# q and k of the later batches: cast on ACT, through a DRAM scratch, read back by transposing DMAs

## The chip, the cores and the metric

The kernel runs on one core of a Trainium2 chip. The metric is the time of one execution on the device in microseconds; the median of several runs is given with the lowest and the highest. A profile records one more execution, instruction by instruction; its span runs from the first instruction to the last and is a little shorter than the time of that execution.

The core has five engines with a queue of instructions each. PE (TensorE) multiplies matrices and loads weights (PEld); DVE (VectorE), ACT (ScalarE) and POOL (GpSimd) work on elements; SP (SyncE) here only issues DMAs. POOL issues DMAs too. An engine takes the instructions of its queue in order: if one waits, all behind it wait.

## The reference

A sliding-window attention, whose output feeds a two-layer network with an ELU between the layers. There are 8 batches, 8 heads, 576 positions, head size 64 and 2048 hidden units; everything is float32 outside.

```python
scores = scale * np.matmul(q, k.transpose(0, 1, 3, 2))
mask = np.abs(pos[:, None] - pos[None, :]) <= 32
attn = softmax(np.where(mask, scores, -1000000000.0))
attn_out = np.matmul(attn, v)                       # (8, 8, 576, 64)
x = attn_out.transpose(0, 2, 1, 3).reshape(4608, 512)
h = x @ w_in                                        # 512 -> 2048
g = np.where(h > 0.0, h, np.exp(np.minimum(h, 0.0)) - 1.0)
out = g @ w_out                                     # 2048 -> 512
```

## The kernel before, in words

**Attention.** The positions of a batch are cut into nine blocks of 64 queries; the 72 blocks of the eight batches are taken in 36 pairs. A block needs only 128 keys around it, so its scores are one 128 x 64 tile a head. For that, q and k must lie with the head dimension across the partitions. `qT` and `kT` hold them so, as bf16, four pairs of heads side by side, two buffers each, used by even and odd batches. `kT` has 32 zero columns on each side of each head pair's 576 keys.

A pair goes through `scores` (L245: 16 matmuls, then an exp on ACT), `mask` (L262, DVE), `pv` (L271, 16 matmuls with V in `V_e` or its copy shifted by 64 rows, `V_o`), `normalize` (L285, DVE) and a transpose of the result `x_st` into `xT`. The first eight pairs do this last transpose on PE (`x_transpose`, `x_evac`), the others with a transposing DMA on SP's queue (`x_dma`, L315).

**How qT and kT are filled.** `load_qk` (L102) brings q or k of a batch into a float32 tile `f` of 96 partitions, six positions a partition, on SP's queue; there are two such tiles for q and two for k. `cast_qk` (L209) casts one pair of heads to bf16. `transpose_qk` (L221) then transposes it on PE, six times 96 x 128 into one PSUM bank, and an engine copies the bank into `qT` or `kT`. Batches 0 and 1 do this in halves, with casts on DVE and ACT. For batches 2 to 7 (L414 to L423) the cast of each head pair runs on POOL and the evacuation on ACT: eight casts, eight groups of six transposes and eight evacuations a batch.

**V and the weights.** POOL's queue issues the loads of V (`load_v`, L114, five DMAs a batch, which cast to bf16 on the way, three buffers) and of the weights. `rotate_v` (L122) makes `V_o` out of `V_e` with two DMAs on SP's queue.

**The network.** Tokens are taken in 18 tiles of 256, that is two pairs each. A tile has eight steps, and a step has two hidden blocks of 128: `mm1` (L439, eight matmuls of 256 columns, exp on ACT into `e_sb`, minus one on DVE into `m_sb`), `elu` (L458, DVE, into `g_sb`) and `mm2` (L466, four matmuls of 512 columns that add into `psY`). After the last step of a tile, ACT and DVE copy `psY` to `y_sb`, and SP's queue stores it.

**The order of work.** It is written out by hand: the program runs through 144 steps `kk`, and the attention's parts are entered into a table by step and slot. A step of the loop at L487 does, in this order: `elu` of the step before, slot `dve`, `mm1`, slot `mid`, `mm2` of two steps before, slot `end`. That is the order on each engine's queue. From pair 8 on, `scores` of pair `i` is in step 4(i-2)-2, only pair 8 is in step 24; `pv` follows one step later at the end, `normalize` and the x transpose two steps later. The tile's `mm1` starts at step 8t, four steps after its second pair's x transpose was entered.

For batch `b`, `k0` is four times (its first pair minus 2): 28, 44, 64, 80, 100 and 116 for batches 2 to 7. The PE transposes of a head pair are in steps k0-16 to k0-3, two every four steps, and the casts five steps ahead of them; batch 2 has its eight transposes in steps 18 to 25. The loads of `f` of batches 3 to 7 are in steps k0-32 and k0-31, of batch 3 in 18 and 19; the V loads follow one step later, and `rotate_v` is in step k0-4.

Of the kernel before, what the change touches and what calls it, by code (L numbers as in the profile page):

```python
# [10 lines left out]
BF16 = mybir.dt.bfloat16  # L11
# [10 lines left out]
def kernel(  # L22
# [9 lines left out]
    nc = tc.nc  # L32

    B, H, S, D = q.shape
    WIN = 32
# [5 lines left out]
    QB = 64  # L41
    NQB = S // QB
    NPAIR = B * NQB // 2
    HP = H // 2
    SJ = 6
    SP_ = S // SJ
    VS = 5
    VD = D + 1
    KW = S + 2 * WIN

    TT = 256
    NT = N_TOK // TT
# [4 lines left out]
    HALF = STEPS // 2  # L57
# [4 lines left out]
    cpool = ctx.enter_context(tc.tile_pool(name="const", bufs=1))  # L62
    wpool = ctx.enter_context(tc.tile_pool(name="weights", bufs=1))
    lpool = ctx.enter_context(tc.tile_pool(name="loads", bufs=2))
    apool = ctx.enter_context(tc.tile_pool(name="attn", bufs=2))
    xpool = ctx.enter_context(tc.tile_pool(name="xT", bufs=4))
    mpool = ctx.enter_context(tc.tile_pool(name="moe", bufs=3))
    opool = ctx.enter_context(tc.tile_pool(name="outs", bufs=2))


    psum = ctx.enter_context(
# [13 lines left out]
    def ps_tile(shape, dt, tag, name):  # L85
        return pools[tag].tile(shape, dt, tag=tag, name=name)

    qT = [cpool.tile([128, HP, S], BF16, name=f"qT{i}") for i in range(2)]
    kT = [cpool.tile([128, HP, KW], BF16, name=f"kT{i}") for i in range(2)]
    V_e = [cpool.tile([128, VS, H, VD], BF16, name=f"Ve{i}") for i in range(3)]  # L90
    V_o = [cpool.tile([128, VS - 1, H, VD], BF16, name=f"Vo{i}")
           for i in range(3)]
# [6 lines left out]
    WHOLE, HALF_A, HALF_B = (0, SJ), (0, SJ // 2), (1, SJ // 2)  # L99
    qk_f = {}  # L100
# [51 lines left out]
    for i in range(3):  # L152
        nc.vector.memset(V_e[i][:, :, :, D:VD], 1.0)
        nc.vector.memset(V_e[i][0:32, 0], 0.0)
        nc.vector.memset(V_e[i][96:128, VS - 1], 0.0)
        if i < 2:
            nc.vector.memset(kT[i][:, :, 0:WIN], 0.0)
            nc.vector.memset(kT[i][:, :, KW - WIN:KW], 0.0)

    ident = cpool.tile([128, 128], BF16)  # L160
    make_identity(nc, ident)
# [4 lines left out]
    for m in (1, 2, 0, 3, 4):  # L166
# [10 lines left out]
        out=masks, in_=masks, compare_op=ALU.is_ge, fill=0.0,  # L177
        base=0, pattern=[[0, 5], [-1, QB]], channel_multiplier=1)
    nc.gpsimd.affine_select(
        out=masks, in_=masks, compare_op=ALU.is_ge, fill=0.0,  # L180
        base=2 * WIN, pattern=[[0, 5], [1, QB]], channel_multiplier=-1)
    for mi in (0, 4):
        nc.gpsimd.affine_select(
            out=masks[:, mi, :], in_=masks[:, mi, :], compare_op=ALU.is_ge,
            fill=0.0, base=-WIN, pattern=[[0, QB]], channel_multiplier=1)
    nc.gpsimd.affine_select(
        out=masks[:, 3, :], in_=masks[:, 3, :], compare_op=ALU.is_ge,
# [15 lines left out]
    def copy_on(eng, d_, s_):  # L203
        if eng is nc.scalar:
            nc.scalar.copy(d_, s_)  # L205
        else:
            eng.tensor_copy(d_, s_)  # L207

    def cast_qk(b, which, part, hps, eng):  # L209
# [8 lines left out]
        qk_b[b, which, z, hp0] = t  # L218
        copy_on(eng, _bap(t, [t.ap[0], [D, nh], [nh * D, nj], [1, D]]), s_)

    def transpose_qk(b, which, part, hps, evac, tag="t0"):  # L221
        z, nj = part
        src = qk_b.pop((b, which, z, hps[0]))
        nh = len(hps)
        W = 512 if nh > 1 else 1024
        pt = ps_tile([128, nh, W], BF16, tag, "ptx")
        for g in range(nh):
            for j in range(nj):
                nc.tensor.transpose(  # L229
                    pt[:, g, j * SP_:(j + 1) * SP_],  # L230
                    src[:, j, g * 128:(g + 1) * 128], ident[0:SP_, 0:SP_])
        n = SP_ * nj
        if which == 0:
            T, c0 = qT[b % 2], z * n
        else:
            T, c0 = kT[b % 2], WIN + z * n
        d = T[:, hps[0]:hps[0] + nh, c0:c0 + n]
        pitch = d.ap[1][0] if nh > 1 else n
        copy_on(evac,
                _bap(d, [d.ap[0], [pitch, nh], [nj, SP_], [1, nj]]),  # L240
                _bap(pt, [pt.ap[0], [W, nh], [1, SP_], [SP_, nj]]))
# [3 lines left out]
    def scores(i, tag="s"):  # L245
        psS = ps_tile([128, 2, 512], FP32, tag, "psS")
        for z in range(2):
            jb = 2 * i + z
            b, qb = jb // NQB, jb % NQB
            for h in range(H):  # L250
                hp, base = h // 2, 64 * (h % 2)
                nc.tensor.matmul(  # L252
                    psS[:, h % 2, hp * 128 + z * QB:hp * 128 + (z + 1) * QB],
                    lhsT=kT[b % 2][base:base + 64, hp, QB * qb:QB * qb + 128],
                    rhs=qT[b % 2][base:base + 64, hp, QB * qb:QB * (qb + 1)],
                    start=True, stop=True)
        pu = apool.tile([128, H, 2 * QB], BF16, tag="pu")
        nc.scalar.activation(  # L258
            pu, _bap(psS, [psS.ap[0], [1, 1024]]), AX.Exp, scale=SCALE)
        st[i] = [psS, pu, None, None, tag]  # L260
# [59 lines left out]
    def first_pair(b):  # L320
        return NQB * b // 2
# [49 lines left out]
    def at(kk, slot, fn, *args):  # L371
        tasks.setdefault((kk, slot), []).append((fn, args))
# [5 lines left out]
    def pair_at(i, kk):  # L378
        at(kk, "mid", scores, i)
        at(kk + 1, "dve", mask, i)  # L380
        at(kk + 1, "end", pv, i)
        at(kk + 2, "dve", normalize, i)
        at(kk + 2, "end", x_transpose, i)
        at(kk + 3, "dve", x_evac, i)


    for i, tag in ((2, "s"), (3, "u")):
        at(0, "mid", scores, i, tag)
        at(1, "dve", mask, i)
# [7 lines left out]
    for part, kq in ((HALF_A, 8), (HALF_B, 16)):  # L397
        for which in range(2):
            at(kq - 1, "mid", cast_qk, 1, which, part, allh,
               (nc.scalar, nc.vector)[which])  # L400
            at(kq + which, "mid", transpose_qk, 1, which, part, allh,
               nc.scalar, "s")
# [4 lines left out]
    for i in range(8, NPAIR):  # L407
        kk = 24 if i == 8 else HALF * (i - 2) - 2
# [4 lines left out]
        at(kk + 2, "end", x_dma, i)  # L413
    for b in range(2, B):  # L414
        k0 = HALF * (first_pair(b) - 2)
        for n in range(2 * HP):
            if b == 2:
                which, hp, kk, ahead = n // HP, n % HP, 18 + n, 2
            else:
                which, hp = n % 2, n // 2  # L420
                kk, ahead = k0 - 16 + HALF * hp + which, 5
            at(kk - ahead, "mid", cast_qk, b, which, WHOLE, (hp,), nc.gpsimd)
            at(kk, "mid", transpose_qk, b, which, WHOLE, (hp,), nc.scalar)  # L423
        at(k0 - HALF, "mid", rotate_v, b)
        if b >= 3:
            kk = max(k0 - 8 * HALF, 18)
            at(kk, "mid", load_qk, b, 0, WHOLE)
            at(kk + 1, "mid", load_qk, b, 1, WHOLE)
            for m in range(VS):
                at(kk + 2 + m // 3, "mid", load_v, b, m)  # L430
# [97 lines left out]
```

The softmax here doesn't subtract the row's maximum and nothing guards it: scores larger than these inputs give would overflow.

## Time and profile before

| | |
|---|---|
| median of 3 runs | 342.21 us (341.41 to 343.56) |
| profiled execution | 341.63 us, its span 339.9 us |
| PE busy | 308.7 us (91% of the span), 3296 matmuls |
| DVE, ACT, POOL busy | 246.2, 167.3 and 84.3 us |
| PE transposes of q and k | 384, casts of them on POOL 48 of 883 ns |
| evacuations of these on ACT | 52 of 634 ns (128 x 576) |
| casts of 96 x 768 on ACT | 4 of 829 ns |
| hardware queue of SP | 36.25 MB, software queue of POOL 8.92 MB |
| load of q or k of a whole batch | 1152 KB, 9.8 and 9.4 us to landing |
| x transpose by DMA | 28, landing 3.4 us after issue in the median |

How to read it: a line of the profile names the source line (L229), the engine, the tile written and the tiles read. The chain that ended last is followed back from the last instruction, at each step to what released it. Matmuls overlap in the pipeline, so the duration of one is longer than the distance to the next; the chain shows distances. A digit in the slices is the busy share of a fortieth of the span in tenths. The time that a DMA takes to land counts from its issue.

### The profile page before, as it was taken

The page shows a single profiled execution, that of the slowest core. Times are in us where ns is not written, and L with a number is a line of the kernel's source. Part 1 is how long each engine was busy: PE and PEld are TensorE (multiplying, and loading weights), DVE is VectorE, ACT ScalarE, POOL GpSimd, SP SyncE. Part 2 cuts the span into 40 slices and gives each one's busy share as a digit, 9 for nine tenths or more (in the row PEclk, how much of TensorE's full clock was granted, in tenths as well). Part 3 has the DMA queues.
Part 4 walks back from the last instruction along what each step waited for, and adds up shares of the span by engine and source line. Part 5 has one row for each costly group of instructions (what it writes and reads, how often), then busy time and mean ns, then how long its engine had stood idle before and what let it go on. Part 6 is the DMA issues. An engine that isn't in the chain of part 4 may idle for free.

```text
span 339.9 us, 8051 instructions
## 1 busy us (share of the span) xinstructions
PE 308.7 (91%) x3296; PEld 207.4 (61%) x3296; DVE 246.2 (72%) x446; ACT 167.3 (49%) x262; POOL 84.3 (25%) x108
## 2 busy tenths in 40 slices
PE   0347999799799999999999999999999999999994
PEld 0235666566566666666666666666666666666662
DVE  5346667678787777778877888788867777878663
ACT  1624264566545554555555554555555553444331
POOL 8352410085661344034400354021100000000000
PEclk9999999999999999999999999999999999999999
DMA  8999999999998995771949994963202320202011
GB/s 163 187 227 214 218 169 185 218 305 214 131 143 173 216 119 121 174 168 23 188 65 206 178 158 83 225 155 80 79 18 78 80 79 17 77 17 80 15 64 62
DMA packets 79176, 45.67 MB, mean 134 GB/s; under 512 B 53796, under 2 KB 73252, under 8 KB 79140
## 3 DMA queue, kind: packets, MB, share of 16 engines
q1 hardware_dynamic: 37412, 36.25, 47.4%
q0 software_dynamic: 41728, 8.92, 37.9%
q8 instruction: 26, 0.43, 0.6%
q14 instruction: 10, 0.08, 0.1%
HBM read 36.70 MB, written 9.44 MB: 136 GB/s over the span
## 4 chain that ended last, share of the span: by engine, by line
PE 83%; DVE 7%; DMA 4%; ACT 3%; issue 1%; SPq 0%; DVEq 0%
PE ps L447 36%; PE psY L474 35%; PE ptx L229 5%; PE psS L279 4%; PE psS L252 3%; DMA f<-in_k_dram 2%; DVE g_sb L460 2%; DMA Vo<-Ve 2%; DVE m_sb L455 1%; ACT e_sb L453 1%; DVE x_st L291 1%; ACT pu L258 1%; ACT qkb L205 1%; DVE pm L267 1%; DVE xT L313 1%
## 5 line engine op out<-in xcount | busy, mean ns | idle before, releaser
L453 ACT ACTIVATE e_sb<-ps 128x512 f32<-128x512 f32 x144 | 86.0, 597 | 152.1 <-PE ps L447 151.9
L447 PE MATMUL ps<-xT,w_in_sb 128*128 128x256 bf16 x1152 | 150.5, 274 | 4.1 <-DVE xT L313 3.3
L474 PE MATMUL psY<-w_out_sb,g_sb 128*128 128x512 bf16 x576 | 148.0, 379 | 0.2 <-DVE g_sb L460 0.2
L447 PEld LDWEIGHTS <-w_in_sb 128*128 128x128 bf16 x1152 | 110.2, 98 | 41.2 <-issue 4.8
L455 DVE TENSOR_SCALAR m_sb<-e_sb 128x512 bf16<-128x512 f32 x144 | 71.9, 500 | 59.2 <-ACT e_sb L453 58.8
L460 DVE SCALAR_TENSOR_TENSOR g_sb<-ps,m_sb 128x512 bf16<-128x512 f32 x144 | 99.4, 690 | 13.0
L474 PEld LDWEIGHTS <-g_sb 128*128 128x128 bf16 x576 | 50.8, 98 | 38.0 <-DVE g_sb L460 0.7
L207 POOL CAST qkb<-f 96x768 bf16<-96x768 f32 x48 | 41.3, 883 | 120.0 <-DMA f<-in_q_dram 40.0
L118 POOL DMA_DIRECT2D Ve<-in_v_dram x40 | 34.8, 875 | 28.1 <-PE psS L279 13.6
L229 PE MATMUL ptx<-ident,qkb 96*128 96x96 bf16 x384 | 27.7, 215 | 15.0 <-DVE qkb L207 12.5
L258 ACT ACTIVATE pu<-psS 128x1024 bf16<-128x1024 f32 x36 | 36.5, 1019 | 2.7 <-PE psS L252 2.6
L229 PEld LDWEIGHTS <-qkb 96*128 96x128 bf16 x384 | 23.5, 102 | 17.3 <-DVE qkb L207 13.0
L267 DVE TENSOR_TENSOR pm<-pu,masks 128x1024 bf16<-128x1024 bf16 x36 | 26.0, 721 | 2.0 <-ACT pu L258 1.7
L291 DVE TENSOR_TENSOR x_st<-psS,rc 128x512 bf16<-128x512 f32 x36 | 24.9, 692 | 1.2
L279 PEld LDWEIGHTS <-pm 128*64 128x64 bf16 x576 | 12.5, 113 | 17.3 <-DVE pm L267 13.4
L205 ACT COPY qT<-ptx 128x576 bf16<-128x576 bf16 (+1 forms) x30 | 20.0, 666 | 4.1 <-PE ptx L229 4.1
L252 PE MATMUL psS<-qT,kT 64*128 64x64 bf16 x576 | 15.3, 196 | 2.7 <-DVE x_st L291 1.2
L205 ACT COPY kT<-ptx 128x576 bf16<-128x576 bf16 (+1 forms) x26 | 17.4, 671 | 0.0
L252 PEld LDWEIGHTS <-kT 64*128 64x128 bf16 x576 | 11.2, 98 | 10.2 <-issue 7.7
L279 PE MATMUL psS<-Ve,pm 128*64 128x65 bf16 x320 | 16.5, 200 | 0.9 <-ACT pu L258 0.6
L279 PE MATMUL psS<-Vo,pm 128*64 128x65 bf16 x256 | 14.5, 200 | 2.0 <-DMA Vo<-Ve 1.9
L483 DVE COPY y_sb<-psY 128x512 f32<-128x512 f32 x18 | 12.4, 687 | 2.2 <-PE psY L474 1.8
(29 smaller groups left out, 55.1 us busy)
## 6 DMA issues: line engine op xcount, KB each, us to landing
out_dram<-y_sb SPq DMA_DIRECT2D x18, 512.0 KB, 2.9
f<-in_q_dram SPq DMA_DIRECT2D x6, 1152.0 KB, 9.8
f<-in_k_dram SPq DMA_DIRECT2D x6, 1152.0 KB, 9.4
Vo<-Ve SPq DMA_DIRECT2D x12, 260.0 KB, 4.0
Ve<-in_v_dram POOLq DMA_DIRECT2D x24, 128.0 KB, 10.9
f<-in_q_dram SPq DMA_DIRECT2D x4, 576.0 KB, 10.3
f<-in_k_dram SPq DMA_DIRECT2D x4, 576.0 KB, 12.0
w_in_sb<-in_moe_w_in_dram POOLq DMA_DIRECT2D x4, 512.0 KB, 19.2
```

The costliest lines, as they stand in the source:

```text
L118: nc.gpsimd.dma_start(out=V_e[b % 3][p0:p1, m, :, 0:D], in_=v[b, :, lo + p0:lo + p1, :].rearrange("h p d -> p h d"))
L205: nc.scalar.copy(d_, s_)
L207: eng.tensor_copy(d_, s_)
L229: nc.tensor.transpose(pt[:, g, j * SP_:(j + 1) * SP_], src[:, j, g * 128:(g + 1) * 128], ident[0:SP_, 0:SP_])
L252: nc.tensor.matmul(psS[:, h % 2, hp * 128 + z * QB:hp * 128 + (z + 1) * QB], lhsT=kT[b % 2][base:base + 64, hp, QB * qb:QB * qb + 128], rh ...
L258: nc.scalar.activation(pu, _bap(psS, [psS.ap[0], [1, 1024]]), AX.Exp, scale=SCALE)
L279: nc.tensor.matmul(psS[QB * z:QB * (z + 1), par, hp * VD:(hp + 1) * VD], lhsT=pm[:, par * HP + hp, z * QB:(z + 1) * QB], rhs=vv[:, qb // 2 ...
L447: nc.tensor.matmul(ps[:, j, :], lhsT=w_in_sb[:, do, fo * 128:(fo + 1) * 128], rhs=xT[t][:, :, do, :], start=(do == 0), stop=(do == NDO - 1))
L453: nc.scalar.activation(e_sb, ps, AX.Exp)
L455: nc.vector.tensor_scalar(m_sb, e_sb, -1.0, None, ALU.add)
L460: nc.vector.scalar_tensor_tensor(g_sb, psH.pop(kk), 0.0, m_t.pop(kk), ALU.max, ALU.min)
L474: nc.tensor.matmul(psY[t][ts], lhsT=g_sb[:, j, ts * 128:(ts + 1) * 128], rhs=w_out_sb[:, s * FG + j, :], start=(s == 0 and j == 0), stop=( ...
```

## The change

For batches 2 to 7, q and k no longer pass through PE. Per operand and batch:

- four casts on ACT (`cast_rows`), a pair of heads each, from `f` into one bf16 tile `rows` of 96 partitions x six positions x 512 columns, so that each position is a row over all heads;
- one DMA on SP's queue (`write_rows`) from `rows` to a DRAM tile of 576 x 512, two buffers each for q and k;
- one transposing DMA on SP's queue (`transpose_rows`) from the DRAM tile into `qT` or `kT`, 128 partitions x four head pairs x 576.

Casts of q stand at the end of steps k0-20 to k0-17, of k four steps later; the write one step after the last cast, the transpose two steps after the write. In batch 2 there are two casts a step, of q in steps 16 and 17, of k in 18 and 19; the writes are in steps 18 and 20, the transposes in 20 and 22. POOL has no casts any more. `kT` becomes one row with the four head pairs side by side, 576 columns apart, which a transposing DMA can fill; the zero columns before and behind are 32 each, and the inner columns of a pair's neighbours are masked. Batches 0 and 1 are as before.

```diff
-    kT = [cpool.tile([128, HP, KW], BF16, name=f"kT{i}") for i in range(2)]
+    KPAD = 2 * WIN
+    kT = [cpool.tile([128, KPAD + HP * S + KPAD], BF16, name=f"kT{i}")
+          for i in range(2)]
...
-            nc.vector.memset(kT[i][:, :, 0:WIN], 0.0)
-            nc.vector.memset(kT[i][:, :, KW - WIN:KW], 0.0)
+            for c0, n in ((KPAD - WIN, HP), (KPAD + HP * S, 1)):
+                z = kT[i][:, c0:c0 + WIN]
+                nc.vector.memset(_bap(z, [z.ap[0], [S, n], [1, WIN]]), 0.0)
...
+    def cast_rows(b, which, hp):
+        if hp == 0:
+            rows[b, which] = lpool.tile([SP_, SJ, H * D], BF16,
+                                        tag=f"r{which}", name="rows", bufs=1)
+        n = SJ * D
+        s_ = qk_f[b, which][:, 2 * hp * n:(2 * hp + 2) * n]
+        d_ = rows[b, which][:, :, 2 * hp * D:(2 * hp + 2) * D]
+        nc.scalar.copy(
+            _bap(d_, [d_.ap[0], [D, 2], [H * D, SJ], [1, D]]),
+            _bap(s_, [s_.ap[0], [n, 2], [D, SJ], [1, D]]))
+
+    def write_rows(b, which):
+        t = dpool.tile([S, H * D], BF16, tag=f"d{which}", name="in_dram")
+        in_dram[b, which] = t
+        nc.sync.dma_start(
+            out=t.rearrange("(p j) c -> p j c", j=SJ), in_=rows.pop((b, which)))
+
+    def transpose_rows(b, which):
+        nc.sync.dma_start_transpose(
+            out=keys_or_queries(b, which), in_=in_dram.pop((b, which)))
...
-        for n in range(2 * HP):
-            if b == 2:
-                which, hp, kk, ahead = n // HP, n % HP, 18 + n, 2
-            else:
-                which, hp = n % 2, n // 2
-                kk, ahead = k0 - 16 + HALF * hp + which, 5
-            at(kk - ahead, "mid", cast_qk, b, which, WHOLE, (hp,), nc.gpsimd)
-            at(kk, "mid", transpose_qk, b, which, WHOLE, (hp,), nc.scalar)
+        for which in range(2):
+            c0 = 16 + 2 * which if b == 2 else k0 - 20 + 4 * which
+            for hp in range(HP):
+                at(c0 + (hp // 2 if b == 2 else hp), "end",
+                   cast_rows, b, which, hp)
+            w0 = c0 + (2 if b == 2 else 4)
+            at(w0, "end", write_rows, b, which)
+            at(w0 + 2, "end", transpose_rows, b, which)
```

More of the change, by code (lines that the diff above doesn't have):

```diff
@@ L48 @@
     VD = D + 1
-    KW = S + 2 * WIN
     TT = 256
@@ L68 @@
     opool = ctx.enter_context(tc.tile_pool(name="outs", bufs=2))
+    dpool = ctx.enter_context(
+        tc.tile_pool(name="dram", bufs=2, space=bass.MemoryType.DRAM))
     psum = ctx.enter_context(
@@ L219, in cast_qk, with keys_or_queries @@
         copy_on(eng, _bap(t, [t.ap[0], [D, nh], [nh * D, nj], [1, D]]), s_)
+    def keys_or_queries(b, which):
+        if which == 0:
+            return qT[b % 2]
+        return kT[b % 2][:, KPAD:KPAD + HP * S].rearrange(
+            "p (g s) -> p g s", g=HP)
+    rows, in_dram = {}, {}
+    def cast_rows(b, which, hp):
[16 more added lines that the diff above has]
+            out=keys_or_queries(b, which), in_=in_dram.pop((b, which)))
     def transpose_qk(b, which, part, hps, evac, tag="t0"):
@@ L232, in transpose_qk @@
         n = SP_ * nj
-        if which == 0:
-            T, c0 = qT[b % 2], z * n
-        else:
-            T, c0 = kT[b % 2], WIN + z * n
-        d = T[:, hps[0]:hps[0] + nh, c0:c0 + n]
+        d = keys_or_queries(b, which)[:, hps[0]:hps[0] + nh, z * n:(z + 1) * n]
         pitch = d.ap[1][0] if nh > 1 else n
@@ L253, in scores @@
                     psS[:, h % 2, hp * 128 + z * QB:hp * 128 + (z + 1) * QB],
-                    lhsT=kT[b % 2][base:base + 64, hp, QB * qb:QB * qb + 128],
+                    lhsT=kT[b % 2][base:base + 64, KPAD + hp * S + QB * qb - WIN:
+                                   KPAD + hp * S + QB * qb - WIN + 128],
                     rhs=qT[b % 2][base:base + 64, hp, QB * qb:QB * (qb + 1)],
@@ L415 @@
         k0 = HALF * (first_pair(b) - 2)
-        for n in range(2 * HP):
-            if b == 2:
-                which, hp, kk, ahead = n // HP, n % HP, 18 + n, 2
-            else:
-                which, hp = n % 2, n // 2
-                kk, ahead = k0 - 16 + HALF * hp + which, 5
-            at(kk - ahead, "mid", cast_qk, b, which, WHOLE, (hp,), nc.gpsimd)
-            at(kk, "mid", transpose_qk, b, which, WHOLE, (hp,), nc.scalar)
+        for which in range(2):
[6 more added lines that the diff above has]
+            at(w0 + 2, "end", transpose_rows, b, which)
         at(k0 - HALF, "mid", rotate_v, b)
```

## The prediction

> **What bounds the kernel now.** I read the busy shares first, then the chain that ended last, then that chain piece by piece.
>
> ```profile
> PE 83%; DVE 7%; DMA 4%; ACT 3%; issue 1%; SPq 0%; DVEq 0%
> ...
> 163.56 0.98 PE ps L447 x8
> 164.54 0.26 PE ptx L229 x6
> 164.80 0.87 PE psY L474 x4
> 165.67 0.87 PE ps L447 x8
> 166.54 0.26 PE ptx L229 x6
> 166.80 0.86 PE psY L474 x4
> ...
> 304.48 0.98 PE ps L447 x8
> ...
> 312.36 0.98 PE ps L447 x8
> ```
>
> TensorE is the bound: from about 97 us on one piece begins where the last ends. A group of six transposes takes 0.26 us of that chain (43 ns each; the 206 ns of the costliest-groups table is latency, overlapped). Four steps take 8.39 us with two groups in them (155.17 to 163.56) and 7.88 us in the tail, where no q or k is left (304.48 to 312.36): 0.51 = 2 x 0.26. No other engine holds the gain back there.
>
> The other resource is the DMA engines, in the slices of the page (8.5 us each), and the queues that feed the second and third batch:
>
> ```profile
> DMA  8999999999998995771949994963202320202011
> ```
>
> ```profile
> 69.16 3.13 POOL L207 CAST qkb<-f 96x768 bf16<-96x768 f32 x4 [21.84 <-PE psY L474]
> 72.61 0.82 POOL L207 CAST qkb<-f 96x768 bf16<-96x768 f32 x1 [0.32 <-DMA f<-in_k_dram]
> 81.37 0.90 POOL L207 CAST qkb<-f 96x768 bf16<-96x768 f32 x1 [1.47 <-DMA f<-in_q_dram]
> ```
>
> ```profile
> 70.70 0.46 SPq L109 DMA_DIRECT2D f<-in_q_dram  x1
> 71.21 1.46 SPq L109 DMA_DIRECT2D f<-in_k_dram  x1
> ```
>
> They are 90% busy or more until 136 us but for two slices at 80%, and mostly idle only after 238. q of batch 2 is cast as it lands (issued 52.4, 16.6 us to landing: 69.0), k at 72.6, q of batch 3 at 81.3. Pair 9, the first that needs batch 2, is step 26; its score matmuls start at 93.43 (PE's timeline), 22 us after k landed.
>
> **What the Trainium skill says.** "DMA: Bandwidth & Descriptors", § Two DMAs through the same engine are not ordered: a DMA that reads what another wrote must be issued after a wait for the first one's semaphore. So the transpose waits in SP's queue for the write to land, and all behind it waits too. SP's waits show such a pair: the V rotations waited 25.9 us for V loads. Same page, § Queues, rings and completion order: on each DMA engine a queue's descriptors are consumed in ring order. The trace agrees: an x transpose lands in 2.4 us at best, 6.4 at worst with loads ahead. Same page, § Latency and other measured facts: 261 GB/s for a DMA transpose with a non-contiguous middle dimension. The trace shows less, from SBUF: 131 KB of x took 0.65 us of all engines (share 0.89 and 0.41 of two half microseconds), 200 GB/s.
>
> **The change part by part**, against the profiled run (341.63 us, span 339.9).
>
> *Removed from PE:* 6 batches x 8 groups x 0.26 = 12.5 us; 10.4 us of it in batches 3 to 7, at the packed places above. The 2.1 us of batch 2 lie in steps 18 to 25, which are rebuilt below.
>
> *ACT:* loses 48 evacuations x 634 ns = 30.4, gains 48 casts x 829 ns (the row of ACT's own casts of this shape) = 39.8. From batch 3 on, eight steps with a cast each hold 8 x 0.60 exp + 8 x 0.83 + 2 x 1.02 + 0.60 = 14.1 us of ACT in 15.8 us of PE. I price it at zero: g_sb is wanted two steps after its exp. Without that cover the fullest step, exp, pu and a cast, is 2.45 us against 1.97: 0.5 us a batch.
>
> *POOL and DVE:* 41.3 us of casts go. m_sb takes 0.43 us alone, up to 1.29 beside them; worth nothing on the path, PE does not wait for it there. But the V loads lose what stood before them on POOL: those of batch 3, issued at 73 to 78 us behind the casts, now go out as soon as batch 2's allow, about 50 to 60. A batch of V is 4608 packets, at 2746 in 3 us (121 to 124, V alone) 5 us of the engines, now in competition with q and k of batch 2: q lands about 71.5, k about 77.
>
> *DMA added, per batch and operand:* a write of 0.59 MB, at the out stores' 390 GB/s 1.5 us, say 1.7, landing 3 us after issue. A transpose of 0.59 MB, nowhere in the trace with a DRAM source: 4.5 x 0.65 = 2.9 us by the x row, 2.3 by the page's 261 GB/s; I take 2.6. SP is held 1.2 us (an x transpose) to 5.4 (4.5 of them); I take 2.4, or until its data flow if the rings are full. Six batches: 12 x 4.3 = 52 us of engines; hidden later, not in the first 120 us.
>
> *Batch 2, steps 16 to 26.* Its casts stand at steps 16 to 19 on ACT, in order. The first waits for q until 71.5 where exp of step 17 would have run at 68.1. Then: two casts 73.1, exp 73.7, kT evacuation 74.8, y_sb copy 75.4. That copy frees the psY bank that step 18's first matmuls take, so they start at 75.4, not 70.28. Eight steps of about 2.1 us bring pair 9 to 92.5 at the least, 94 with the normalise that it waited for before: even without the DMA, batch 2's gain is gone. SP's order is now out store, f q(3), write q(2), f k(3), transpose q(2), write k(2), transpose k(2). Each f load is 1.18 MB at 230 GB/s (110 to 115 us), 5.1 us. From 77, when k(2) is in: two out stores to 80, f q(3) 85.2, write q 86.9, f k(3) 92, transpose q 94.6, write k 96.3 and landed 97.4, transpose k 98.5 to 101.1, landed 102.1; the V loads of batch 4, which start near 92.5, put some 2 us in. Pair 9 starts at about 104 instead of 93.4: **+10.7**. The V rotations of batch 2, before at 72.9, now stand behind the transpose of k on SP: issued near 102, landed near 107, wanted by pair 9's PV at the end of the next step, about 108. Zero behind this stall; with pair 9 on time they would be late themselves unless SP is free by about 92.
>
> *Batches 3 to 7.* Behind each SP wait for a landed write stand out stores, f loads and x transposes. What can be late is the x transpose at the end of a step that is 4 modulo 8: the tile's first matmul is 4 steps on, 6.2 us after x_st is ready (step = 7.88/4 = 1.97). Batch 3, from the start of step 28 as zero: x(9) issued 1.7; write q 4.0 to 5.7, landed 6.5; transpose q to 10.2; f q(4) 15.3; x(10) 16; write k 17.7; f k(4) 22.8; out 24.2; transpose k 26.8; x(11) 27.5, landed 28.5. Step 40 wants it at 23.6: **+4.9**. Before, x(11) had only f k(4) and the out store ahead. Batch 4 likewise, from step 48: f q(5) is in first; write q 5.7, f k(5) 10.8, out 12.2, transpose q 14.8, x landed 16.5, wanted 15.8: **+0.7**. Batch 5, from step 64: write q 5.2, out 6.6, transpose q 9.7, f q(6) 14.8, x landed 16.5, wanted 15.8: **+0.7**. In batch 6 the tight x lands 22.9 for 23.6, batch 7 has no f load: zero. kT's layout and its zero pads: zero, the same instructions.
>
> Sum: 341.63 + 10.7 - 10.4 + 4.9 + 0.7 + 0.7 = 348.2. The median of the runs shown is 0.6 above the profiled run: **349 us**.
>
> **The rivals.**
> *Faster: the DMA fits.* If the transposed k of batch 2 lands before about 94, because the write and the transpose pass the f loads instead of queueing behind them, pair 9 loses nothing, and x(11) is in time too: 342.2 - 10.4 to 12.5 = 330 to 332. For it: 22 us between k's landing and pair 9. Against: engines at 9 throughout, one queue, two waits for landings in it. It decides at pair 9's start: every microsecond past 94 costs one, and from 104.5 the gain is gone.
> *About even.* V of batch 3 does no harm (q at 69.0, k at 72.6). ACT's queue still puts step 18 at 73; the chain ends at 98: +5, with batch 3 at +4 and the rest zero: 342.2 - 10.4 + 9 = 341.
> *Slower still.* The DRAM source makes a transpose 5 us, or SP is held 5.4: two in batch 2, two in batch 3, one each in 4 and 5, 2.4 more each: 349 + 14 = 363.
> *ACT is the bound:* exps late in each cast stretch, five times 0.5, 351.5. Against it: 1.7 us of 15.8 are free. I keep it in the main case's width.
> That the change does not do what it says cannot be: 288 transposes are not issued.
>
> **How the numbers follow.** Main case (344 to 358) 0.54, faster (328 to 337) 0.20, about even (337 to 345) 0.18, slower still (358 to 368) 0.08. One per cent, 338.8 to 345.6, is about what a measurement of this kernel can tell from no change. From the cases: faster 0.23, same 0.17, slower 0.60. The range 332 to 359 leaves out about 0.08 at each end; the main case's own is 344 to 358.
>
> **What would show it.** Right: a wait of PE's score matmuls for a transposing DMA into kT of some 10 us near 100 us; step 18 started late behind ACT; one wait of 3 to 6 us for xT at step 40; otherwise four steps in 7.88 us; SP waiting for in_dram to land. Wrong: no PE wait over 2 us at pair 9 (then 331); waits of ps for e_sb or g_sb in the cast stretches (ACT); a transpose of 0.59 MB far from 2.6 us; xT late in every batch, not in one.

## The result, and the profile after

The changed kernel takes 376.81 us in the median (372.18 to 377.97); the kernel before, on the same chip, 341.81 us (340.98 to 343.56). The ratio is 1.097, with a 95% interval of 1.086 to 1.108; it leaves out the slow execution of 377.97. The kernel is slower, by much more than the 349 us that were forecast, and outside the range of the forecast. The profiled execution took 376.67 us with a span of 374.9.

The busy shares of the chain that ended last, the clock slices and the DMA slices of the changed kernel (9.4 us a slice):

```profile
PE 62%; DMA 27%; DVE 2%; SPq 2%; ACT 2%; issue 2%; DVEq 0%; ACTq 0%
...
PEclk9999999879769985999879998999999999999998
DMA  8999999999969999399973899879984782022211
```

PE's part of the chain falls from 83% to 62%, that of the DMAs rises from 4% to 27%. New too: in several slices between the eighth and the twenty-fifth TensorE is not granted its full clock (5 to 8 tenths). The DMA engines, 7 or less in most slices from the sixteenth on before, are now at 8 or more in most of them up to the thirtieth.

What PE's matmuls waited for, in the whole execution (total, times, longest), and what SP's queue waited for:

```profile
PE ps L480 <- DMA xT<-x_st: 25.2, 4, 11.5
PE psS L284 <- DMA kT<-in_dram: 9.3, 1, 9.3
PE ps L480 <- ACT y_sb L515: 3.2, 1, 3.2
```

```profile
SPq L254 <- DMA in_dram<-rows: 57.4, 12, 13.9
```

The second and the third line are the two waits that the prediction had in batch 2: 9.3 us of pair 9 for the transposed k, and step 18 behind the psY copy on ACT. The first is the surprise: four waits of a tile's first matmul for a transpose of x that stands behind the new DMAs in SP's queue, 25.2 us, where one of 4.9 and two of 0.7 were forecast.

To see where each microsecond came from, I compared the start of every step's first exp in the two traces (lateness: after less before).

| stretch | lateness at its end, us | change, us | forecast, us |
|---|---|---|---|
| to step 16 | 0.35 | +0.4 | 0 |
| steps 17 to 28 (batch 2, pair 9) | 13.71 | +13.4 | +10.7 |
| step 40 (12.16 at 39, 25.80 at 41) | 25.80 | +13.6 | +4.9 |
| step 56 (24.51 to 33.88) | 33.88 | +9.4 | +0.7 |
| step 72 (32.07 to 37.97) | 37.97 | +5.9 | +0.7 |
| step 96 (35.38 to 37.25) | 37.25 | +1.9 | 0 |
| all other steps after 28, together | | -9.8 | -10.4 |
| end | 34.67 | 34.7 | 6.6 |

34.7 is all but 0.3 us of the difference of the spans (374.9 - 339.9 = 35.0). The gain is there, as priced: in steps 28 to 39, to take one stretch, the lateness falls in pieces of 0.26 us. It is paid for four and a half times over.

The chain of the changed kernel through step 40, the costliest place (start, duration, what):

```profile
121.94 10.50 DMA in_dram<-rows
...
132.50 8.23 SPq L254
...
140.79 4.95 DMA xT<-x_st
...
145.78 1.89 PE ps L480 x8
147.67 1.71 PE psY L507 x4
```

k of batch 3 is written at 121.94 and landed 10.5 us later; the transpose of it then holds SP for 8.23 us; only after that can SP issue the x transpose, which takes 4.95. And the matmuls that had waited for it run at half speed: 1.89 and 1.71 us for groups that take 0.87 and 0.86 elsewhere.

SP's queue in the same stretch shows what lies ahead of that transpose:

```profile
119.60 0.57 SPq L114 DMA_DIRECT2D f<-in_q_dram  x1
120.26 1.58 SPq L350 DMA_TRANSPOSE xT<-x_st  x1
121.94 0.79 SPq L250 DMA_DIRECT2D in_dram<-rows  x1
122.78 0.50 SPq L114 DMA_DIRECT2D f<-in_k_dram  x1
123.37 3.13 SPq L517 DMA_DIRECT2D out_dram<-y_sb  x1
132.50 8.23 SPq L254 DMA_TRANSPOSE kT<-in_dram  x1
140.79 1.26 SPq L350 DMA_TRANSPOSE xT<-x_st  x1
```

The load of k of batch 4 was issued at 122.78 and landed 15.6 us later, at 138.4: the transpose's own packets lie behind it on the engines. That leaves several causes for one delay: batch 2's late start, the wait for a landed write, the loads ahead of it, V's loads beside it, the sheer number of bytes. The experiments take them one by one. The working theory was "order in SP's queue"; the rivals "landed writes", "more bytes than the engines can carry" (by the prediction's durations and the transposes' 2.9 us, an estimate, the DMAs of a batch add up to some 33 of its 36 us) and "everything follows from batch 2".

### The profile page after: what moved, and what is told of

The parts are those of the page before. It is cut to its first block, busy times and chain, and to the rows that moved or that the text cites. A ratio compares the mean times of both kernels' runs of the same rounds, so it can differ in the third digit from the quotient of the medians.

```text
span 374.9 us, 7397 instructions
## 1 busy us (share of the span) xinstructions
PE 305.0 (81%) x2961; PEld 199.9 (53%) x3008; DVE 235.1 (63%) x446; ACT 175.7 (47%) x262; POOL 42.9 (11%) x60
## 4 chain that ended last, share of the span: by engine, by line
PE 62%; DMA 27%; DVE 2%; SPq 2%; ACT 2%; issue 2%; DVEq 0%; ACTq 0%
PE ps L480 30%; PE psY L507 27%; DMA Ve<-in_v_dram 9%; DMA xT<-x_st 6%; DMA f<-in_q_dram 5%; DMA in_dram<-rows 4%; PE psS L284 3%; PE psS L312 3%; SPq L254 2%; DMA f<-in_k_dram 2%; DMA kT<-in_dram 1%; ACT e_sb L486 1%; DVE g_sb L493 1%; DVE m_sb L488 1%; PE ptx L265 0%
## 5 line engine op out<-in xcount | busy, mean ns | idle before, releaser
L480 PE MATMUL ps<-xT,w_in_sb 128*128 128x256 bf16 x1152 | 157.3, 282 | 32.0 <-DMA xT<-x_st 25.2
L480 PEld LDWEIGHTS <-w_in_sb 128*128 128x128 bf16 x1152 | 113.4, 101 | 73.5 <-issue 19.6
L507 PE MATMUL psY<-w_out_sb,g_sb 128*128 128x512 bf16 x529 | 143.3, 389 | 3.3 <-issue 1.1
L488 DVE TENSOR_SCALAR m_sb<-e_sb 128x512 bf16<-128x512 f32 x144 | 61.9, 430 | 97.0 <-ACT e_sb L486 95.4
L507 PEld LDWEIGHTS <-g_sb 128*128 128x128 bf16 x576 | 54.5, 100 | 41.4 <-issue 3.3
L291 ACT ACTIVATE pu<-psS 128x1024 bf16<-128x1024 f32 x36 | 36.5, 1019 | 10.6 <-PE psS L284 10.5
L243 ACT CAST rows<-f 96x768 bf16<-96x768 f32 x48 | 39.2, 824 | 1.1 <-DMA f<-in_q_dram 1.1
L300 DVE TENSOR_TENSOR pm<-pu,masks 128x1024 bf16<-128x1024 bf16 x36 | 24.6, 683 | 10.9 <-ACT pu L291 10.7
L284 PE MATMUL psS<-qT,kT 64*128 64x64 bf16 x576 | 15.7, 199 | 10.4 <-DMA kT<-in_dram 9.3
L284 PEld LDWEIGHTS <-kT 64*128 64x128 bf16 x576 | 11.5, 100 | 18.1 <-DMA kT<-in_dram 9.5
L265 PE MATMUL ptx<-ident,qkb 96*128 96x96 bf16 x96 | 7.5, 243 | 15.3 <-DVE qkb L213 12.9
L265 PEld LDWEIGHTS <-qkb 96*128 96x128 bf16 x96 | 6.1, 117 | 16.4 <-DVE qkb L213 13.5
L515 ACT COPY y_sb<-psY 128x512 f32<-128x512 f32 x18 | 10.5, 582 | 2.0 <-PE psY L507 2.0
L321 DVE RECIPROCAL rc<-psS 128x8 f32<-128x8 f32 x36 | 7.1, 199 | 2.0 <-PE psS L312 2.0
```

The costliest lines, as they stand in the source:

```text
L243: nc.scalar.copy(_bap(d_, [d_.ap[0], [D, 2], [H * D, SJ], [1, D]]), _bap(s_, [s_.ap[0], [n, 2], [D, SJ], [1, D]]))
L284: nc.tensor.matmul(psS[:, h % 2, hp * 128 + z * QB:hp * 128 + (z + 1) * QB], lhsT=kT[b % 2][base:base + 64, KPAD + hp * S + QB * qb - WIN: ...
L291: nc.scalar.activation(pu, _bap(psS, [psS.ap[0], [1, 1024]]), AX.Exp, scale=SCALE)
L300: nc.vector.tensor_mul(pm, pu, _bap(mm, [mm.ap[0], [0, H], [1, 2 * QB]]))
L480: nc.tensor.matmul(ps[:, j, :], lhsT=w_in_sb[:, do, fo * 128:(fo + 1) * 128], rhs=xT[t][:, :, do, :], start=(do == 0), stop=(do == NDO - 1))
L488: nc.vector.tensor_scalar(m_sb, e_sb, -1.0, None, ALU.add)
```

## The experiments

A time with a range is the median of four executions; the other experiments ran once. The four executions of the changed kernel lie up to 5.8 us apart (372.18 to 377.97), so where two single times differ by less, only the waits and steps of their traces are compared.

**x transposes back on PE.** From pair 9 on, x is transposed by matmuls (pair 8 keeps its DMA; with its transpose on PE too, this order of work deadlocks), so nothing that PE soon wants stands behind the new DMAs except qT and kT.

```diff
-        at(kk + 2, "end", x_dma, i)
+        if i == 8:
+            at(kk + 2, "end", x_dma, i)
+            continue
+        at(kk + 2, "end", x_transpose, i)
+        at(kk + 3, "dve", x_evac, i)
```

> The changed kernel, but from pair 9 on x is transposed on PE, not by a DMA. Theory (the x transposes are late because they stand in SP's queue and in its DMA rings behind the new writes and transposes): the four waits of the first matmuls for xT, 30.8 us with the slow clock after them, go; 27 more groups of four PE transposes of 0.24 us cost 6.5; batch 2's loss of some 15 stays: 352 us. Rival (the DMA engines have too many bytes to move, whatever the order): q and k arrive late instead, 365 us or more. Rival (ACT is the bound): no change, 375.

352.75 us, before 341.39. The waits for xT are gone; scores still wait for kT, 12.8 us in two waits. Of the two, 11.2 us are pair 9's in batch 2; the other, 1.6 us, is that of the first scores of batch 3, at step 42. The lateness is 13.7 us at step 28 and 10.95 at the end. So the transposes into qT and kT of batches 3 to 7 are themselves in time but for these 1.6 us: nearly all that is lost there is lost by the x transposes that share their queue.

**Batch 2 back on PE.** Batch 2's casts return to POOL and its transposes to PE; batches 3 to 7 stay changed.

```diff
-        for which in range(2):
-            c0 = 16 + 2 * which if b == 2 else k0 - 20 + 4 * which
+        for n in range(2 * HP if b == 2 else 0):
+            at(16 + n, "mid", cast_qk, b, n // HP, WHOLE, (n % HP,), nc.gpsimd)
+            at(18 + n, "mid", transpose_qk, b, n // HP, WHOLE, (n % HP,),
+               nc.scalar)
+        for which in range(2 if b > 2 else 0):
+            c0 = k0 - 20 + 4 * which
...
```

> The changed kernel, but batch 2 takes the old way (casts on POOL, PE transposes in steps 18 to 25); batches 3 to 7 as changed. Theory (batch 2's loss has its own causes, ACT waiting for q and the transposed k coming at 104.9): steps 17 to 19 lose nothing, pair 9 starts near 94, so 15.1 us go and 2.1 of PE come back; the xT waits at steps 40, 56, 72 and 96 stay: 362 to 364 us. Rival (the early stall only gives the DMAs time that is then missing later): the xT waits grow by most of it, 370 us or more.

363.43 us, before 341.78. Until step 39 the kernel is level with the one before (-0.65 us there). Then the same four waits come:

```profile
PE ps L484 <- DMA xT<-x_st: 25.1, 4, 11.1
```

25.1 against 25.2 us. "Everything follows from batch 2" falls: the two losses are separate and add up. Batch 2 is worth some 13 us of the 35.

**Loads of q and k on POOL's queue**, first alone, then with batch 2 on PE. SP's queue loses the long loads; the idea was that the transposes then go out and land at once.

```diff
-        nc.sync.dma_start(
+        (nc.gpsimd if b >= 3 else nc.sync).dma_start(
             out=t[:, z * n:(z + 1) * n].rearrange("p (h x) -> p h x", h=H),
```

> The changed kernel, but the loads of f of batches 3 to 7 are issued on POOL's queue, not on SP's; same bytes, same steps. Theory (order in one queue): writes, transposes and x no longer stand behind 1.18 MB loads, so the xT waits shrink from 25 us to under 5 and the wait for kT at pair 9 from 9.3 to about 3: 345 us, between 340 and 352. Rival (total DMA work decides): within 8 us of 376. Rival (SP's wait for the landed write alone): about half, 360.

> Both edits: batch 2 the old way and f of batches 3 to 7 on POOL's queue. Theory: nothing waits for a DMA any more; the kernel before less 10.4 us for 40 groups of PE transposes, 332 us, up to 336 if one x is still late. Rival (total DMA work): 355 or more.

Both forecasts missed by far. Alone: 385.13 us (kT wait 17.6, xT waits 27.4). With batch 2 on PE: 375.35 (374.23 to 376.97), before 341.78, ratio 1.096 (1.091 to 1.101), slower than the 363.43 of the run without this edit. SP's queue and the DMA issues of the second of them:

```profile
112.34 12.37 SPq L254 DMA_TRANSPOSE qT<-in_dram  x1
124.81 1.22 SPq L350 DMA_TRANSPOSE xT<-x_st  x1
```

```profile
qT<-in_dram SPq DMA_TRANSPOSE x5, 13.4
```

With no load ahead of it in its own queue, a transpose now holds SP for 12.37 us, and those into qT take 13.4 us to land in the median (8.8 in the changed kernel). The one at 112.34 moved its first packet 6.4 us after its issue and its last 11.4 us after that; with nothing in the way it is 1.3 and 2.6 to 2.9 us. "DMA: Bandwidth & Descriptors", § Queues, rings and completion order, says that each DMA engine goes round robin between the queues it has work for, a packet at a time. The trace agrees with it. This is what POOL's queue (q0, the loads of q and k) and SP's queue (q1, this transpose) moved from 119 to 123 us, in packets, MB and share of the 16 engines:

```profile
q0 software_dynamic: 196, 0.90, 96.8%
q1 hardware_dynamic: 192, 0.05, 8.9%
```

The queues take turns, packet for packet, but a packet of the load has 4.6 KB and one of the transpose 256 bytes, so the transpose gets one byte in nineteen. (256 bytes is its packet size throughout: the changed kernel has 28,224 more packets under 512 bytes than the one before, and twelve transposes of 0.59 MB in such packets would be 27,648.) What kept its first packet back for 6.4 us is not shown by this. In any case another queue is no escape: the engines are shared.

**Casts on POOL.** Only the engine of the new casts is changed back.

```diff
-        nc.scalar.copy(
+        nc.gpsimd.tensor_copy(
```

> The changed kernel with its casts on POOL, not on ACT. Theory (ACT costs only at steps 17 to 19, where its queue waits for q of batch 2, 4.9 us, and what is won there is then waited for at pair 9 for kT): 371 to 376 us, kT some 3 us earlier than 104.9, xT waits as before. Rival (ACT's eight casts a batch hold up exps and buffers everywhere): 355 to 362.

373.2 us, before 341.39. Steps 17 to 19 are now in time (0.64 us early at step 19), and step 27 is 9.2 us late instead of 13.4; the xT waits stay, 24.0 us. So ACT's queue costs time in batch 2, and in sum nothing later. How much is not sharp: step 28 is 9.2 us late here, 13.7 in the changed kernel, but 11.0 in the run without waits for landed writes below, whose batch 2 is also cast on ACT; that makes 1.7 to 4.5 us. From step 39 to the end the two kernels lose about the same (23.5 us here, 22.5 with the casts on ACT), though here in six waits for xT and there in four.

**Loads of q and k entered later, batch 2 on PE.** The loads of a batch move to 9 and 7 steps before the previous batch's first pair, so that they no longer lie just before this batch's transposes.

```diff
-            at(kk, "mid", load_qk, b, 0, WHOLE)
-            at(kk + 1, "mid", load_qk, b, 1, WHOLE)
+            kf = 18 if b == 3 else HALF * (first_pair(b - 1) - 2) - 9
+            at(kf, "mid", load_qk, b, 0, WHOLE)
+            at(kf + (1 if b == 3 else 2), "mid", load_qk, b, 1, WHOLE)
```

> Batch 2 the old way, as in the run of 363.4 us; besides, the loads of f of batches 4 to 7 stay on SP's queue but are entered after the transpose of k of the batch before, at its k0-9 and k0-7, so that no load stands between a write, its transpose and the next x. Theory (what delays x is the 1.18 MB loads in the same rings, ahead of the write that SP waits for and of the transpose ahead of x): no xT wait over 1 us; the kernel before less 10.4: 332 us, up to 335. Rival (the wait for the landed write and the transpose alone delay x, loads or not): three xT waits of 5 us or more are left, 345 to 355.

362.67 us, before 341.39, ratio 1.060 (1.055 to 1.065). About what batch 2 on PE gave alone (363.43). Its profile is of an execution of 368.3 us, so the order of events is read from it and not the total. The long hold of SP by the transpose of k of batch 3 is gone (2.82 us), but at step 40:

```profile
117.48 1.42 SPq L114 DMA_DIRECT2D f<-in_q_dram  x1
119.00 2.46 SPq L350 DMA_TRANSPOSE xT<-x_st  x1
```

```profile
119.00 11.81 DMA xT<-x_st
```

The x transpose that PE wants next now has a 1.18 MB load directly ahead of it, and lands 11.81 us after its issue. The load had been taken from before one transpose and put before another.

**No wait for landed writes.** The scratch rows of batches 3 to 7 are still written, but their transposes read batch 2's scratch, which has long landed and has buffers of its own here. Same bytes, same order, no wait; q and k of the later batches are left out and replaced by those of batch 2.

```diff
...
-            out=keys_or_queries(b, which), in_=in_dram.pop((b, which)))
+            out=keys_or_queries(b, which), in_=in_dram[2, which])
```

> The changed kernel, but the transposes of batches 3 to 7 read the scratch of batch 2, which landed long before, so that SP waits for no write there; writes, loads and transposes are all issued. q and k of those batches are thereby those of batch 2. Theory (the rings' contents decide, since SP is held until a transpose's data are near their end): the transpose of k at step 40 still stands behind f of k, x comes 2 to 4 us earlier there and at steps 56 and 72: 366 to 371 us. Rival (SP's wait for the landing decides): the xT waits fall below 3 us each, 350 or less.

365.32 us, before 341.39; the xT waits fall from 25.2 to 17.4 us. The landed-write wait is a third of the waits for xT, not more. SP's queue at step 40 shows why:

```profile
119.71 0.52 SPq L114 DMA_DIRECT2D f<-in_k_dram  x1
120.33 0.82 SPq L518 DMA_DIRECT2D out_dram<-y_sb  x1
121.20 14.99 SPq L255 DMA_TRANSPOSE kT<-in_dram  x1
136.29 1.22 SPq L351 DMA_TRANSPOSE xT<-x_st  x1
```

The transpose is issued 11.3 us earlier than in the changed kernel and lets SP go only 4.5 us earlier, of which 2.8 are a lead that this kernel has already at step 39: it holds the queue for 14.99 us while the loads ahead of it run. Here the wait was mostly standing in for transfers that were in the way in any case.

**No V loads for batches 4 to 7.**

```diff
-            for m in range(VS):
+            for m in range(VS if b == 3 else 0):
```

> The changed kernel without the loads of V of batches 4 to 7 (V_e keeps the V of batches 1 to 3 there; the V rotations are left in). Theory (V is 5 us of small packets a batch in the other ring, which slow what is ahead of x): the xT waits with their slow clock fall from 30.8 to 15 to 20 us: 360 to 366. Rival (the V loads, now sent one by one after each pair, are what makes x late): under 5 us are left, 350 or less. Rival (SP's own order alone): 373 or more.

363.8 us, before 343.28; xT waits 16.4, kT wait 6.9. By steps: 7.8 us are lost at step 40 instead of 13.6, 4.1 at step 56 instead of 9.4, but 6.3 at step 72 and 4.4 at step 96, where it was 5.9 and 1.9. At step 72 the x transpose, with a load of q directly ahead, lands 9.60 us after its issue without any V in the way, 10.03 with it. So V's loads lengthen the first two stalls and not the other two.

**No loads of q and k of batch 3.** Batch 3 uses the `f` tiles of batch 1. This asks whether batch 2's stall was the two loads ahead of its transposes in SP's queue.

```diff
-            at(kk, "mid", load_qk, b, 0, WHOLE)
-            at(kk + 1, "mid", load_qk, b, 1, WHOLE)
+            if b == 3:
+                qk_f[3, 0], qk_f[3, 1] = qk_f[1, 0], qk_f[1, 1]
+            else:
+                at(kk, "mid", load_qk, b, 0, WHOLE)
+                at(kk + 1, "mid", load_qk, b, 1, WHOLE)
```

> The changed kernel without the two loads of f of batch 3; its casts read the q and k of batch 1 that are in SBUF. Theory (k of batch 2 is late at pair 9 because two 1.18 MB loads stand in the rings between its write and its transpose): the transposed k lands at 92 to 95 instead of 104.9, the wait of 9.3 at pair 9 goes to 1 or less, the later xT waits stay within 3 us each: 364 to 368 us. Rival (the two waits of SP for a landed write and the V loads keep k late by themselves): a wait of 5 us or more is left at pair 9, 372 or more.

360.79 us, before 343.11. SP's queue:

```profile
87.43 2.65 SPq L254 DMA_TRANSPOSE kT<-in_dram  x1
```

k of batch 2 is landed 4.7 us after this issue, at 92.1, and pair 9 does not wait: step 28 is 0.2 us early. In the changed kernel the same transpose was issued at 100.10. Batch 2's stall is these two loads, as the prediction had it. The later stalls stay (xT 22.6 us).

**Another order, nothing else.** Batch 2 on PE; the rest has the same DMAs. Every x transpose that PE wants within a tile goes first, the transpose into qT or kT directly behind one, a load of q or k behind that; the writes stand four steps ahead of their transposes, the casts earlier to suit. `tk` is the step of a batch's transpose of k, that of q stands eight steps ahead of it; both are steps that are 4 modulo 8.

```diff
...
+        tk = k0 - 8 if k0 % 8 == 4 else k0 - 12
+        at(k0 - HALF, "mid" if k0 % 8 == 4 else "end", rotate_v, b)
+        for which in range(2 if b > 2 else 0):
+            t0 = tk - 8 + 8 * which
             for hp in range(HP):
-                at(c0 + (hp // 2 if b == 2 else hp), "end",
-                   cast_rows, b, which, hp)
-            w0 = c0 + (2 if b == 2 else 4)
-            at(w0, "end", write_rows, b, which)
-            at(w0 + 2, "end", transpose_rows, b, which)
-        at(k0 - HALF, "mid", rotate_v, b)
+                at(22 + hp // 2 if (b, which) == (3, 0) else t0 - 8 + hp,
+                   "end", cast_rows, b, which, hp)
+            at(t0 - 4, "end", write_rows, b, which)
+            at(t0, "end", transpose_rows, b, which)
+        loads = {2: (18, 19, 3), 3: (28, 36, 4), 4: (44, 52, 5),
+                 5: (68, 76, 6), 6: (84, 92, 7)}
...
```

> Batch 2 the old way; in batches 3 to 7 everything long on SP's queue (transpose, then load of f) is entered directly after an x transpose at a step that is 4 modulo 8, the writes four steps earlier after the other x, casts earlier to match. So the x with 6 us to its use always comes first, and only the x with 14 us of it stands behind long DMAs; a write has 8 us to land before SP waits for it. Same DMAs, same bytes. Theory (x is late by what is entered ahead of it in one queue, and by nothing else): no xT wait over 1 us, 332 us, up to 335. Rival (the engines are too full: 33 us of DMA work by its own durations in the 36 us of a batch, so some DMA is late in any order): xT or Vo waits of 10 us or more in all, 347 to 360.

335.26 us (333.33 to 336.48), before 343.28, ratio 0.977 (0.971 to 0.983). This decides between order and bytes. The packets and bytes of batch 2 on PE, and then of this kernel:

```profile
DMA packets 103655, 57.45 MB, mean 159 GB/s; under 512 B 77316, under 2 KB 96772, under 8 KB 103620
```

```profile
DMA packets 103655, 57.45 MB, mean 172 GB/s; under 512 B 77316, under 2 KB 96772, under 8 KB 103620
```

The two move the same packets to the byte and differ by 28.2 us (363.43 and 335.26). "More bytes than the engines can carry" falls. The granted clock is 0.995 on the mean, and PE's waits for DMAs are now small ones:

```profile
PE psS L312 <- DMA Vo<-Ve: 3.9, 3, 1.5
...
PE ps L488 <- DMA xT<-x_st: 0.9, 1, 0.9
```

**The V rotations four steps earlier too**, from batch 3 on.

```diff
-        at(k0 - HALF, "mid" if k0 % 8 == 4 else "end", rotate_v, b)
+        at(k0 - (HALF if b == 2 else 2 * HALF), "end", rotate_v, b)
```

> The order of the run of 335.3 us, but the V rotations of batches 3 to 7 four steps earlier, directly after the x of step k0-8 and ahead of the transpose there, because pair k0-2's PV waited for V_o 3.9 us in all. Theory: these waits go, 331 to 332.5 us. Rival (the room on the queue is used up, and what comes earlier makes another late): 335 or more, with xT waits of 2 us or more.

334.34 us (333.29 to 335.62), before 343.11, ratio 0.978 (0.972 to 0.985). The Vo wait halves (1.9 us in one), and 1.5 us of xT waits take part of its place. The median is 0.9 us lower than that of the run before, but on another chip and with overlapping ranges: a difference that is not shown. Either order is faster than the kernel before by about 2.2%; the intervals of the two reach from 1.5 to 2.9%. With batch 2 also through the DRAM scratch neither order was run.

All waits are PE's, from the one execution that was profiled:

| | us | before, same chip | waits for kT | waits for xT |
|---|---|---|---|---|
| the change | 376.81 | 341.81 | 9.3 | 25.2 |
| x on PE | 352.75 | 341.39 | 12.8 | 0 |
| batch 2 on PE | 363.43 | 341.78 | 0 | 25.1 |
| loads on POOL | 385.13 | 341.78 | 17.6 | 27.4 |
| both of these | 375.35 | 341.78 | 0 | 37.4 |
| casts on POOL | 373.2 | 341.39 | 10.5 | 24.0 |
| loads later, batch 2 on PE (profile of 368.3 us) | 362.67 | 341.39 | 0 | 19.7 |
| no wait for writes | 365.32 | 341.39 | 9.3 | 17.4 |
| no V of 4 to 7 | 363.8 | 343.28 | 6.9 | 16.4 |
| no q, k loads of 3 | 360.79 | 343.11 | 0 | 22.6 |
| other order | 335.26 | 343.28 | 0 | 0.9 |
| other order, V rotations too | 334.34 | 343.11 | 0.5 | 1.5 |

## Why the prediction was wrong

The side was right; the size was not: 349 forecast, 376.8 measured, above the range.

**PE's saving: right.** 0.26 us a group; 9.8 of the 10.4 us forecast for batches 3 to 7 are seen outside the stalled steps.

**Batch 2: right in mechanism, 2.7 us short.** q landed at 69.4 (forecast 71.5) and step 18 began at 73.03 (forecast 75.4; the "about even" rival had 73). V's earlier loads did less harm than priced. Step 19 was still 5.2 us late, where 5.1 had been priced, but by luck: 2.8 us came from ACT, and the rest from matmuls at half clock after PE's wait (granted clock 0.50 from 73.03 to 78.88), which the prediction did not have. The chain to k's transpose came out as worked: landed at 104.9 for a forecast of 102 to 104. PE's timeline there:

```profile
104.93 0.61 PE L284 MATMUL psS<-qT,kT 64*128 64x64 bf16 x16 [9.26 <-DMA kT<-in_dram]
```

Forecast 104. What was missing is that PE came out of this stall too at half clock: the next groups of eight and four matmuls took 1.71 and 1.18 us, not 0.87 and 0.86. The 2.7 us are themselves not sharp: the same stretch cost 11.0 us in the run without waits for landed writes. The cause that the prediction named, two loads ahead in one queue, is shown by the run without them.

**Transposes of 0.59 MB: right.** Where nothing was ahead, SP was held 2.5 us and the packets took 2.6 to 2.9 us (2.6 was taken). The rival "slower still" came nearest in time (363), but half by luck. A transpose of 5 us is not there; its other half, SP held 5.4 us, is: five of the twelve transposes held it 5.9 to 9.5 us, all with other DMAs under way. The main case had allowed for that ("until its data flow if the rings are full") and given it no time.

**ACT and POOL: right** to price the casts at zero in batches 3 to 7, in sum (23.5 and 22.5 us from step 39 on, casts on POOL and on ACT).

**The failed step is "Batches 3 to 7".** It forecast +4.9, +0.7, +0.7, 0 and 0, in all 6.3 us; the jumps were 13.6, 9.4, 5.9 and 1.9, in all 30.8. One of its own signs of being wrong, "xT late in every batch, not in one", all but came up: xT was late in four of the five. It named the right instruction, the x transpose at the end of a step that is 4 modulo 8, and the right steps. Beginning with step 28 as zero (110.6 us), forecast and trace agree up to the load of q (issued 9.0; forecast 6.5 + 2.4), and then part:

| batch 3, us from step 28 | forecast | trace |
|---|---|---|
| write of q landed | 6.5 | 6.6 |
| write of k landed (forecast: through at 17.7, 0.8 more to landing, as for q) | 18.5 | 21.8 |
| load of k of batch 4 in (trace: landed) | 22.8 | 27.8 |
| transpose of k through (trace: SP free of it) | 26.8 | 30.1 |
| x(11) landed (wanted 23.6) | 28.5 | 35.1 |

The last line differs by 6.6 us; with 2.1 us of matmuls at half clock after the wait it makes the 8.7 between 4.9 and 13.6. Three terms of the sum were too small.

1. *The rate of the queue.* q, x, the write and k are 3.1 MB. From the issue of the first (9.0) the forecast had the last in by 22.8, after 13.8 us; in the trace it landed after 18.8 (119.60 to 138.4). The forecast had 230 to 390 GB/s for SP's queue and no V beside it, though V's packets go to the same engines (from 132 to 137 us POOL's queue moved 651 packets, V's, beside 683 of SP's). Without V the same four took 15.9 us (113.67 to 129.5). V is the first part, 5.8 of 13.6 us at step 40 and 5.2 of 9.4 at step 56.
2. *A transfer behind a load.* I let an x transpose start when the load ahead had its bytes through at the rate of a load alone, 5.1 us. At step 72 the x transpose with one load of q directly ahead took 10.03 us to land from its issue, and 9.60 with V left out. From the end of the transpose of q (216.0) it took 9.2, where the forecast had 6.8. The term was priced at the average rate of all sixteen engines, but x landed only when the last of them was done, and one was late. By 223.35 all but 33 of the 512 packets of x had been moved. This is the window after that (its last three figures are the granted clock, the DMA share and GB/s):

```profile
223.35:224.15 0.80, 0.00 (x0) 0.00 (x0) 0.00 (x0) 0.00 (x0) 0.00 (x0) 1.00 0.06 15
```

The share of 0.06 is one engine in sixteen; it moved eight packets of the load, one after the other. The 33 packets of x followed from 224.21 to 224.66 (a sixteenth of 512 is 32), and x landed at 225.19. The late engine is 1.3 of the 2.4 us between 6.8 and 9.2; the rest stays open.

3. *Half clock after a stall*, in no part of the forecast: the four jumps add to 30.8 us, PE's waits for xT to 25.2; the 5.6 us between them go with matmuls at half clock after the first three.

The wait for a landed write, which the prediction put first, is about 8 of the 25 us of waits; with another order of the queue nearly all of them go (0.9 us left). In batches 4, 5 and 6 the sum came out within 0.7 us of the deadline. That should have been read as "no slack left", with the cost bounded upward by a load that takes longer, and not as a value near zero; the range had no case for it.

The faster rival, 330 to 332 us, was nearer to what the change can do than it looked: with the order changed and batch 2 left on PE the time is 335.26 and 334.34.

## What to carry to other kernels

When a transfer is moved into a queue that already feeds the bound engine, write out the queue's order and ask of every transfer that this engine waits for what is directly ahead of it: here the same packets in two orders differed by 28 us. A small urgent transfer goes before the large one, not behind it, and a transfer that has to wait for another is issued so late that the wait is already over. A second queue on the same engines did not help a transfer in small packets here, and slack that comes out at zero is to be priced as a loss.

## What the runs showed of the hardware that had not been expected

**Half clock after a stall.** PE's windows of the changed kernel after the stall of step 40 (window, length, busy time and count of PE, PEld, DVE, ACT, POOL, granted clock, DMA share, GB/s):

```profile
145.70:147.70 2.00, 1.92 (x9) 1.34 (x10) 0.00 (x0) 0.00 (x0) 0.00 (x0) 0.50 1.02 195
147.70:149.30 1.60, 1.60 (x5) 0.59 (x4) 0.86 (x2) 0.60 (x1) 0.00 (x0) 0.50 0.17 23
...
151.00:152.00 1.00, 1.00 (x7) 0.61 (x7) 0.45 (x2) 1.00 (x2) 0.00 (x0) 1.00 0.00 0
```

"TensorE: Matmul & The Clock Gate", § What's actually happening: the array is throttled to half its clock by default, and after an idle window of about 3.4 us, until about 3.4 us of sustained activity release it. The trace agrees: after the stall of 11.5 us the clock is 0.50 for 4.8 us more, and full from 150.6 on. The stalls of 7.4 and 4.4 us at steps 56 and 72 are followed by half clock too, the one of 1.8 us at step 96 is not. The first three cost 1.5 to 2.1 us each on top of their length. A shorter idle stretch than the page's was enough as well: the wait of 3.2 us at step 18 (0.50 until 78.88), and in the run without waits for landed writes one of 2.2 us (0.50 from 72.42 to 75.83).

**An issue can hold SP for long.** A transposing DMA of 0.59 MB held SP for 2.2 us at best, 8.23 behind a load in the same queue, 12.37 beside loads in another, and 14.99 where its wait for the write was taken away. All that time nothing behind it was issued.

**A small transfer behind a large one.** With a load directly ahead, 131 KB of x took 9.6 to 11.8 us to land, where 5.1 us of load and 0.65 of its own are what the average rates give. At step 72 part of the difference is one DMA engine that was 1.3 us behind the fifteen others.

**Turns by packet, not by bytes.** In the run with the loads on POOL's queue and batch 2 on PE, two queues moved 196 and 192 packets in 4 us, and 0.90 and 0.05 MB.
